# Token-major attention output, accumulated logits and ranks, and later expert weights in a fused attention and mixture-of-experts kernel

## The chip, the cores and the metric

The kernel runs on one core of one Trainium2 chip. The metric is the device time of one execution in microseconds; less is better. Engines: PE (TensorE), DVE (VectorE), ACT (ScalarE), POOL (GpSimd), SP (SyncE).

## The reference

Three parts, one after the other, in FP32:

```python
# decayed linear attention, B, H, S, D = 4, 8, 768, 64
state = gamma * state + k_t v_t^T        # per batch and head
y_t = scale * q_t state
# top-1 mixture of experts on x = y as [3072, 512]; 8 experts, 512 -> 1024 -> 512
logits = x @ w_gate
e_idx = argmax(logits)                   # first of equal ones
gate_w = softmax(logits)[e_idx]
eom = sigmoid(x @ w_output_gate)[e_idx]
x = gate_w * eom * (relu(x @ w1[e_idx]) @ w2[e_idx])
# RMS norm and a gated block, 512 -> 1536 -> 512
out = (silu(xn @ w_gate2) * (xn @ w_val)) @ w_out
```

## The kernel before, in words

The 3072 tokens are cut into 24 chunks of 128, six to a batch. A loop over chunks `n` (L672) runs the attention stage. In iteration `n`, PE does in this order: the scores of chunk n+1 (`qk`, L467: eight matmuls on 64 rows each, the two heads of a pair on two halves of the array), the rows and logits of chunk n-1 (`rows`, L524), the state product of chunk n (`qs_pv`, L490, not in a batch's first chunk), its value product (L495), the state update (`st_up`, L513, not in a batch's last chunk), and the ranks of chunk n-1 (`place`, L555 to L557).

The attention output is feature-major: a head pair's 128 features lie on the partitions and the 128 tokens along the row. `rows` therefore multiplies each of its four blocks with a constant of 144 columns, 128 of the identity and 16 of the two gate matrices. That gives the row of each token and four partial logits, which DVE adds (L529). DVE then finds the largest logit, the first expert that has it, and its one-hot row; `run_cnt` (L544) sums one-hot rows over the chunks. `place` makes the rank of each token within its expert by three small matmuls, weighs the row (L588), stores it to DRAM from ACT's queue, and scatters the token's number into a list by an indirect DMA on POOL.

In FP32 every PE.matmul shows as two LDWEIGHTS (PEld) and two MATMUL records. Expert weights come in 64 pieces of 512 KB; a piece is split into a high and a low half by ACT (L179) and POOL (L180). Eight pieces are loaded and split while the attention stage runs, one in every second chunk (L690 to L692, L704). In the expert loop `convs_to` (L861) asks for further pieces. SP issues nearly all loads in program order, and q, k and v of a chunk use one of four buffers, so a load waits for the chunk four before it.

The rows of the first expert window are collected in two ways: tokens of early chunks are gathered from DRAM (`gather`, L255, four indirect DMAs on POOL) and added by PE with the identity (`settle_in`, L604); tokens of the last three chunks (NDIRECT) are put in place by matmuls with a selection matrix, as a rounded part `rh` and a rest `rl` (`direct_in`, L595). Then `split` (L263, L264) makes the two halves that the first expert's `up` (L285) reads.

The order of the work on each engine is the order in which the code issues it; the tile framework adds the waits. The end of the stage reads:

```python
        direct_in(NCH - 3, True)
        place(NCH - 2)
        rows(NCH - 1)
        settle_in((0, 1))
        place(NCH - 1)
        settle_in((2, 3))
        direct_in(NCH - 2, False)
        direct_in(NCH - 1, False)
```

Of the kernel before, what the change touches and what calls it, by code (L numbers as in the profile page):

```python
# [21 lines left out]
CH = 128  # L22
# [21 lines left out]
NDIRECT = 3  # L44
# [27 lines left out]
def shape_constants():  # L72
# [14 lines left out]
    hd = 2 * np.arange(NP)[None, None, :, None] + (p[:, None, None, None] >= 64)  # L87
    ti = np.arange(CPB)[None, :, None, None] * CH + p[None, None, None, :] + 1.0
    rs = g[hd] ** ti / np.sqrt(D)
# [14 lines left out]
def fused_kernel(  # L104
# [311 lines left out]
    with ExitStack() as es:  # L416
# [3 lines left out]
        rp = pool(es, "rowp", 4)  # L420
# [11 lines left out]
        st_sb = [ap.tile([128, NP, 128], F32, name=f"st{i}") for i in range(2)]  # L432
        run_cnt = ap.tile([128, NCH + 1, NE], BF16, name="run_cnt")
# [3 lines left out]
        a_t, vt_t, am_t, xt_t, row_t, rt, direct = {}, {}, {}, {}, {}, {}, {}  # L437
        scat = []
# [44 lines left out]
        def qs_pv(n):  # L483
            c = n % CPB
            qT = a_t[n][:, 0].rearrange("p (a t) -> p a t", a=NP)
            vt, am = vt_t[n], am_t.pop(n)
            o = ps[:, 4].rearrange("p (a t) -> p a t", a=NP)
            if c:
                for a in range(NP):
                    PE.matmul(  # L490
                        o[:, a], lhsT=st_sb[n % 2][:, a], rhs=qT[:, a], start=(a == 0), stop=True, skip_group_check=True
                    )
            for a in range(NP):
                for i in range(2):
                    PE.matmul(  # L495
                        o[64 * i:64 * i + 64, a], lhsT=vt[:, 2 * a + i], rhs=am[i][:, a],
                        start=(c == 0 and a == 0), stop=True, skip_group_check=True,
                    )
            xt = tp.tile([128, NP, CH], F32, name="xt", tag="xt")
            DVE.tensor_tensor(out=xt, in0=o, in1=rs[:, c], op=ALU.mult)  # L500
            xt_t[n] = xt

        def st_up(n):
# [16 lines left out]
        def rows(n):  # L520
            xt = xt_t.pop(n)
            for k in range(KB):
                o = (k % 2) * 144
                PE.matmul(ps[:, 5 + k // 2, o:o + 144], lhsT=xt[:, k], rhs=iwt[:, k], start=True, stop=True)  # L524
            v = ps[:, 5:7, 0:288].rearrange("p a (b c) -> p a b c", b=2)
            t = rp.tile([128, DM], F32, name="row", tag="row")
            row_t[n] = t
            lg = tp.tile([128, 16], F32, name="lg", tag="lg")
            DVE.tensor_reduce(  # L529
                out=lg, in_=v[:, :, :, 128:144].rearrange("p a b j -> p j a b"), axis=AX.XY, op=ALU.add  # L530
            )
            ACT.activation(
                out=t.rearrange("p (a b c) -> p a b c", a=2, b=2), in_=v[:, :, :, 0:128], func=AF.Copy
            )
            sc = tp.tile([128, 12], F32, name="sc", tag="sc")
            col = [sc[:, i:i + 1] for i in range(12)]
            mx, pm, nmx, sm, nz, ez, s1, t1, gw, pos = col[:10]
            ohb = tp.tile([128, NE], BF16, name="ohb", tag="ohb")
            DVE.tensor_reduce(out=mx, in_=lg[:, 0:8], axis=AX.X, op=ALU.max)
            DVE.scalar_tensor_tensor(out=junk[:, 0], in0=lg[:, 0:8], scalar=mx, in1=prio, op0=ALU.is_ge, op1=ALU.mult)  # L540
            DVE.tensor_scalar(out=nmx, in0=mx, scalar1=-1.0, scalar2=None, op0=ALU.mult)
            DVE.tensor_reduce(out=pm, in_=junk[:, 0], axis=AX.X, op=ALU.max)
            DVE.tensor_scalar(out=ohb, in0=prio, scalar1=pm, scalar2=None, op0=ALU.is_equal)
            DVE.tensor_tensor(out=run_cnt[:, n + 1], in0=run_cnt[:, n], in1=ohb, op=ALU.add)  # L544
            ACT.activation(out=junk[:, 1], in_=lg[:, 0:8], func=AF.Exp, bias=nmx, accum_out=sm)
            DVE.scalar_tensor_tensor(
                out=junk[:, 2], in0=lg[:, 8:16], scalar=-1.0, in1=ohb, op0=ALU.mult, op1=ALU.mult, accum_out=nz
            )
            ACT.activation(out=ez, in_=nz, func=AF.Exp)
            rt[n] = (ohb, ez, sm, s1, t1, gw, pos)  # L550

        def place(n):
            ohb, ez, sm, s1, t1, gw, pos = rt.pop(n)
            rk = ps[:, 7, (n % 2) * 8:(n % 2) * 8 + 8]
# [20 lines left out]
            if n < NCH - 1:  # L575
                store_row(n, t, gw)
            else:
                row_t[n] = (t, gw)
# [30 lines left out]
        def totals_a():  # L609
            PE.matmul(ps[:, 7, 32:40], lhsT=oh, rhs=run_cnt[:, NCH], start=True, stop=True)  # L610
# [456 lines left out]
```

## Time and profile before

| | |
|---|---|
| three runs | 1118.16, 1119.85, 1119.85 us; median 1119.85 |
| the profiled execution | 1119.29 us, of which the span is 1117.2 us |
| busy share of the span | PE 94%, PEld 88%, DVE 49%, ACT 34%, POOL 30% |
| mean granted clock | 0.986 |

Times in the rows are microseconds from the start of the span, means are nanoseconds. "out<-in" names the tiles; "L500" is a line of the kernel. PE and PEld overlap: PEld is the load of the stationary operand, PE the stream of the moving one. The engines' idle time is put down to what ended it. The attention stage ends at about 153 us, the experts run from 173 us on, and the last block from about 460 us to the end.

### The profile page before, as it was taken

The numbers are of one execution on the slowest core, as the hardware profiler recorded it, in microseconds if no ns is written. First come the engines' busy times: TensorE is split into PE (matmuls) and PEld (weight loads), VectorE is DVE, ScalarE is ACT, GpSimd is POOL, SyncE is SP. The second block draws the span as 40 slices with busy tenths as digits, with TensorE's granted clock in tenths as the row PEclk, the third lists the DMA queues.
The fourth block names the chain that finished last, engine by engine and source line by source line (L and its number), as shares of the span: only waits on it lengthen the run. The fifth ranks groups of instructions, "written<-read, shape, count | busy, mean of one in ns | idle before, by whom it ended". The sixth has DMA issues, their size and how long they took to land.

```text
span 1117.2 us, 16379 instructions
## 1 busy us (share of the span) xinstructions
PE 1055.5 (94%) x6393; PEld 982.8 (88%) x6394; DVE 550.9 (49%) x1045; ACT 381.4 (34%) x721; POOL 337.2 (30%) x271
## 2 busy tenths in 40 slices
PE   7788889999999999989899899999999999999995
PEld 6687779989999999978788799999999999999995
DVE  4699963256666676888888831111311112211111
ACT  1344333444444544555555531111311112211111
POOL 3355544556466656332433310000110000200002
PEclk9899989999999999999999999999999999999998
DMA  8999724445446555543343220000210000100001
GB/s 301 229 307 284 204 63 135 123 135 197 155 142 205 182 156 155 171 104 94 114 141 114 85 85 29 1 1 1 64 50 1 1 1 30 57 1 1 1 1 60
DMA packets 47864, 116.74 MB, mean 104 GB/s; under 512 B 12966, under 2 KB 24486, under 8 KB 44962
## 3 DMA queue, kind: packets, MB, share of 16 engines
q1 hardware_dynamic: 39602, 97.05, 28.8%
q0 software_dynamic: 4864, 12.53, 3.2%
q10 hardware_dynamic: 3312, 6.03, 1.6%
q8 instruction: 52, 0.85, 0.3%
q14 instruction: 34, 0.28, 0.1%
HBM read 93.06 MB, written 23.11 MB: 104 GB/s over the span
## 4 chain that ended last, share of the span: by engine, by line
issue 43%; PE 25%; DVE 11%; POOL 3%; DMA 2%; ACT 2%; POOLq 0%; DVEq 0%; SPq 0%; ACTq 0%
PE ps L285 12%; PE ps L298 11%; DVE fb L226 2%; DVE fb L229 2%; POOL out_dram L780 2%; DVE fu L232 1%; DVE fb L223 1%; PE ps L271 1%; DMA out_dram<-ob,perm 1%; DVE a L755 1%; DVE al L757 1%; ACT ah L756 1%; DVE ys L347 1%; PE ps L604 1%; DMA raw<-wm 1%
## 5 line engine op out<-in xcount | busy, mean ns | idle before, releaser
L747 PE MATMUL ps<-zh,w 128*128 128x384 f32 x960 | 255.2, 336 | 2.6 <-DVE hl L292 1.3
L755 DVE TENSOR_TENSOR a<-a,ps 128x384 f32<-128x384 f32 x96 | 52.8, 550 | 320.2 <-PE ps L747 317.7
L180 POOL TENSOR_TENSOR w<-raw,w 128x1024 fp32r<-128x1024 f32 x64 | 154.7, 2426 | 103.0 <-ACT w L179 102.2
L747 PEld LDWEIGHTS ps<-zh,w 128*128 128x128 f32 x960 | 174.6, 188 | 5.7 <-ACT a L754 1.7
L747 PE MATMUL ps<-xh,w 128*128 128x384 f32 x576 | 156.5, 341 | 9.8 <-ACT a L754 7.2
L747 PE MATMUL ps<-zl,w 128*128 128x384 f32 x480 | 161.2, 336 | 0.0
L285 PE MATMUL ps<-xh,w 128*128 128x448 f32 (+7 forms) x512 | 149.6, 353 | 0.1
L765 PE MATMUL ps<-w,ah 128*128 128x512 f32 x564 | 145.5, 393 | 0.2 <-ACT ys L320 0.2
L780 POOL DMA_INDIRECT out_dram<-xw,perm x10 | 9.9, 992 | 423.3 <-ACT xw L778 420.1
L756 ACT ACTIVATE ah<-a 128x384 fp32r<-128x384 f32 x94 | 49.3, 525 | 209.6 <-DVE a L755 209.6
L747 PEld LDWEIGHTS ps<-xh,w 128*128 128x128 f32 x576 | 104.9, 188 | 17.3 <-ACT a L754 11.3
L765 PEld LDWEIGHTS ps<-w,ah 128*128 128x128 f32 x564 | 104.7, 188 | 16.6 <-ACT ys L320 0.6
L754 ACT ACTIVATE a<-ps 128x384 f32<-128x384 f32 x96 | 46.7, 487 | 202.6 <-PE ps L747 202.5
L298 PE MATMUL ps<-hh,w 128*128 128x448 f32 (+7 forms) x512 | 106.6, 350 | 0.0
L285 PEld LDWEIGHTS ps<-xh,w 128*128 128x128 f32 x512 | 95.2, 188 | 3.4
L747 PE MATMUL ps<-xl,w 128*128 128x384 f32 x288 | 96.9, 336 | 0.0
L298 PEld LDWEIGHTS ps<-hh,w 128*128 128x128 f32 x512 | 93.8, 188 | 2.9
L747 PEld LDWEIGHTS ps<-zl,w 128*128 128x128 f32 x480 | 90.1, 188 | 2.3
L285 PE MATMUL ps<-xl,w 128*128 128x448 f32 (+7 forms) x256 | 89.8, 351 | 0.0
L180 POOL TENSOR_TENSOR w<-fu,w 128x512 fp32r<-128x512 f32 x36 | 55.7, 1546 | 111.7 <-ACT w L179 108.2
L765 PE MATMUL ps<-w,al 128*128 128x512 f32 x282 | 80.1, 392 | 0.0
L757 DVE TENSOR_TENSOR al<-a,ah 128x384 fp32r<-128x384 f32 x94 | 52.5, 558 | 55.5 <-ACT ah L756 55.5
(154 smaller groups left out, 1497.9 us busy)
## 6 DMA issues: line engine op xcount, KB each, us to landing
raw<-wmoe SPq DMA_DIRECT2D x64, 512.0 KB, 3.9
qkv<-att SPq DMA_DIRECT2D x22, 1024.0 KB, 8.0
raw<-wm SPq DMA_DIRECT2D x36, 512.0 KB, 3.7
xw<-z SPq DMA_DIRECT2D x8, 768.0 KB, 6.4
xr<-row ACTq DMA_DIRECT2D x23, 256.0 KB, 7.8
z<-ys SPq DMA_DIRECT2D x2, 912.0 KB, 7.6
z<-ys SPq DMA_DIRECT2D x2, 896.0 KB, 4.3
z<-ys SPq DMA_DIRECT2D x2, 864.0 KB
```

The source lines that it names most:

```text
L180: POOL.tensor_tensor(out=dst[:, 1, c], in0=src, in1=f32(dst[:, 0, c]), op=ALU.subtract)
L226: DVE.scalar_tensor_tensor(out=b, in0=lo, scalar=29, in1=b, op0=ALU.logical_shift_right, op1=ALU.bitwise_or)
L229: DVE.scalar_tensor_tensor(out=b, in0=hi, scalar=-(1 << 30), in1=b, op0=ALU.bitwise_and, op1=ALU.bitwise_or)
L285: PE.matmul(p, lhsT=wtile[:, s, k * 128:(k + 1) * 128], rhs=x[w % len(xh)][:, k, 0:n], start=(i == 0), stop=(i == 3 * KB - 1),)
L298: PE.matmul(ps[:, 4 + k, 0:n], lhsT=wtile[:, s, 512 + k * 128:512 + (k + 1) * 128], rhs=h, start=(f == 0 and j == 0), stop=(f == NF - 1 an ...
L747: PE.matmul(ps[:, part, 0:BT], lhsT=w2(f, part, s, k * 128, (k + 1) * 128), rhs=zz[:, k], start=(i == 0), stop=(i == 3 * KB - 1),)
L754: ACT.activation(out=a, in_=ps[:, 0, 0:BT], func=AF.Silu)
L755: DVE.tensor_tensor(out=a, in0=a, in1=ps[:, 1, 0:BT], op=ALU.mult)
L756: ACT.activation(out=ah, in_=a, func=AF.Copy)
L757: DVE.tensor_tensor(out=al, in0=a, in1=f32(ah), op=ALU.subtract)
L765: PE.matmul(ps[:, o_bank[b % 2][t]], lhsT=x[:, t * 128:(t + 1) * 128], rhs=w2(f, 2, s, 0, 512), start=(f == 0 and j == 0), stop=(f == NF2 ...
L780: ins = POOL.indirect_dma_start(out=out[:, :], out_offset=bass.IndirectOffsetOnAxis(ap=pm[:, t0 + t], axis=0), in_=o, in_offset=None, boun ...
```

## The change

The attention output is made token-major. The value product now has the masked scores as its stationary operand (128 columns) and the scaled values (64 columns) as the moving one; the state product has q as the stationary operand and the state, no longer padded to a 128x128 block, as the moving one. DVE scales it straight into the row. For the logits, the row is turned by four transposes (`turn_row`), copied by ACT, and multiplied with 16 columns, the four blocks accumulating in PSUM (`logits`). The logits are negated in the constant, so that the largest becomes the smallest. The ranks of all chunks accumulate in one place in PSUM (`rank`): each chunk adds what the chunk before left out and its own part, and `run_cnt` goes. The row stage takes one more chunk: choosing the expert of chunk n-1 and weighing chunk n-2 are issued on DVE in turn. Chunk n-2 is placed in iteration n. The state is copied whole by ACT. Weight pieces are loaded from chunk 20 on; three are split in the stage, the rest behind the first window. Four chunks instead of three go by `direct_in`, the gather comes in the last iteration, and the last two chunks are ranked before the gathered rows are added.

```diff
-NDIRECT = 3
+NDIRECT = 4
...
-        rp = pool(es, "rowp", 4)
+        rp = pool(es, "rowp", 6)
...
-        rs = ap.tile([128, CPB, NP, CH], F32, name="rs")
-        iwt = ap.tile([128, KB, 144], F32, name="iwt")
+        rs = ap.tile([128, CPB * H], F32, name="rs")
+        iwt = ap.tile([128, KB, 16], F32, name="iwt")
+        rest = ap.tile([128, 128], BF16, name="rest")
-        st_sb = [ap.tile([128, NP, 128], F32, name=f"st{i}") for i in range(2)]
+        st_sb = [ap.tile([128, NP, D], F32, name=f"st{i}") for i in range(2)]
+        ranks = ps[:, 7, 0:8]
...
-            o = ps[:, 4].rearrange("p (a t) -> p a t", a=NP)
+            o = ps[:, 4:6, 0:NP * D].rearrange("p g (a e) -> p g a e", a=NP)
             if c:
-                for a in range(NP):
+                for h in range(H):
+                    r = 64 * (h % 2)
                     PE.matmul(
-                        o[:, a], lhsT=st_sb[n % 2][:, a], rhs=qT[:, a], start=(a == 0), stop=True, skip_group_check=True
+                        o[:, h % 2, h // 2], lhsT=qT[r:r + 64, h // 2], rhs=st_sb[n % 2][r:r + 64, h // 2],
+                        start=(h < 2), stop=True, skip_group_check=True,
                     )
...
+            for h in range(H):
+                PE.matmul(
+                    o[:, h % 2, h // 2], lhsT=am[h % 2][:, h // 2], rhs=vt[:, h], start=(c == 0 and h < 2), stop=True,
+                    skip_group_check=True,
+                )
+            t = rp.tile([128, DM], F32, name="row", tag="row")
+            a = c * H
+            DVE.tensor_tensor(
+                out=t.rearrange("p (a g e) -> p g a e", a=NP, g=2), in0=o,
+                in1=rs[:, a:a + H].rearrange("p (g a o) -> p g a o", g=2, o=1).to_broadcast([128, 2, NP, D]), op=ALU.mult,
+            )
+            row_t[n] = t
...
-            ACT.activation(out=s[0:64, :, 0:64], in_=v[0:64], func=AF.Copy)
-            DVE.tensor_copy(out=s[64:128, :, 64:128], in_=v[64:128])
+            ACT.activation(out=s, in_=v, func=AF.Copy)
+
+        def turn_row(n):
+            x = ps[:, 6].rearrange("p (k t) -> p k t", k=KB)
+            for k in range(KB):
+                PE.transpose(x[:, k], row_t[n][:, k * 128:(k + 1) * 128], ident)
+            xt = tp.tile([128, KB, CH], F32, name="xt", tag="xt")
+            ACT.activation(out=xt, in_=x, func=AF.Copy)
+            xt_t[n] = xt
+
+        def logits(n):
+
             xt = xt_t.pop(n)
+            lg = ps[:, 6, 0:16]
             for k in range(KB):
...
+                PE.matmul(lg, lhsT=xt[:, k], rhs=iwt[:, k], start=(k == 0), stop=(k == KB - 1))
...
+        def rank(n):
+
+            if n:
+                PE.matmul(ranks, lhsT=rest, rhs=rt[n - 1][2], start=False, stop=True, skip_group_check=True)
+            else:
+                PE.matmul(ranks, lhsT=oh[0:1], rhs=e3[0:1], start=True, stop=True, skip_group_check=True)
+            PE.matmul(ranks, lhsT=uh, rhs=rt[n][2], start=False, stop=True, skip_group_check=True)
+
+        def choose(n):
+            lg, sc, ohb = rt[n]
+            nm, pm, sm, nz, ez = [sc[:, i:i + 1] for i in range(5)]
+
+            def chosen():
+                DVE.tensor_scalar(out=ohb, in0=prio, scalar1=pm, scalar2=None, op0=ALU.is_equal)
+                ACT.activation(out=junk[:, 1], in_=lg[:, 0:8], func=AF.Exp, scale=-1.0, bias=nm, accum_out=sm)
+
+            def gate():
+                DVE.scalar_tensor_tensor(
+                    out=junk[:, 2], in0=lg[:, 8:16], scalar=1.0, in1=ohb, op0=ALU.mult, op1=ALU.mult, accum_out=nz
+                )
+                ACT.activation(out=ez, in_=nz, func=AF.Exp)
...
+            if n < NCH - 2:
+                store_row(n)
...
-            if n == NCH - 2:
+            if n == NCH - 1:
                 ex.gather(0, CAPS[0], NT - NDIRECT * CH)
             qk(n + 1)
             if n >= 1:
-                rows(n - 1)
+                turn_row(n - 1)
             qs_pv(n)
+            if n >= 2:
+                rank(n - 2)
+            if n >= 1:
+                logits(n - 1)
             st_up(n)
-            if 1 <= n < NCH - 1:
-                place(n - 1)
-            if n == NCH - 3:
+            in_turn(choose(n - 1) if n >= 1 else [], weigh(n - 2) if n >= 2 else [])
+            if n >= 2:
+                place(n - 2)
+            if n == NCH - NDIRECT + 1:
                 ex.load_list(0, CAPS[0], 0)
-            if n >= 3 and n % 2 == 1:
-                convs_to((n - 3) // 2)
-                loads_to((n - 3) // 2 + 2)
-        direct_in(NCH - 3, True)
+            if n >= NCH - 4:
+                loads_to(n - NCH + 5)
+                convs_to(n - NCH + 4)
+        direct_in(NCH - 4, True)
+        turn_row(NCH - 1)
+        rank(NCH - 2)
+        direct_in(NCH - 3, False)
+        logits(NCH - 1)
+        in_turn(choose(NCH - 1), weigh(NCH - 2))
         place(NCH - 2)
-        rows(NCH - 1)
-        settle_in((0, 1))
+        rank(NCH - 1)
+        in_turn(weigh(NCH - 1))
         place(NCH - 1)
-        settle_in((2, 3))
         direct_in(NCH - 2, False)
-        direct_in(NCH - 1, False)
+        last = CAPS[0] // 128 * 128
+        settle_in(range(0, last, 128))
         for k in range(KB):
+            settle_in(range(last, CAPS[0], 128), (k,))
+            direct_in(NCH - 1, False, (k,))
             ex.split(0, k, CAPS[0], ps[:, k, 0:CAPS[0]])
-        store_row(NCH - 1, *row_t[NCH - 1])
-        convs_to(NPRE)
+        store_row(NCH - 2)
+        store_row(NCH - 1)
...
-            convs_to(min(t + NSLOT - 3, NPRE + max(0, t - 1) * 3 // 2))
+            convs_to(min(t + NSLOT - 3, 4 + t * 3 // 2))
```

## Rows read from the trace of the kernel before

**Rows 1.** Stretches: length; PE, PEld, DVE, ACT, POOL busy; PEclk; DMA; GB/s.

```profile
54.80:116.20 61.40, 51.74 (x701) 46.84 (x698) 57.89 (x200) 27.29 (x69) 32.76 (x35) 1.00 0.97 287
116.20:119.60 3.40, 3.40 (x18) 3.18 (x19) 3.23 (x14) 1.55 (x4) 2.11 (x3) 0.50 0.85 243
157.20:170.80 13.60, 11.62 (x40) 9.48 (x41) 2.37 (x12) 1.69 (x5) 4.48 (x8) 0.50 0.15 46
```

**Rows 2.** One chunk of PE in order of time: start, length, group, instructions.

```profile
22.49 1.16 PE L467 MATMUL ps<-qkv 64*128 64x128 f32 x16
23.59 1.25 PE L524 MATMUL ps<-iwt,xt 128*128 128x144 f32 x8
24.67 1.05 PE L490 MATMUL ps<-qkv,st 128*128 128x128 f32 x8
25.65 1.09 PE L495 MATMUL ps<-am,vt 128*64 128x128 f32 x16
26.58 0.63 PE L513 MATMUL ps<-vt,qkv 128*64 128x64 f32 x16
27.14 0.17 PE L555 MATMUL ps<-e,oh 1*128 1x8 bf16 x1
27.39 1.16 PE L467 MATMUL ps<-qkv 64*128 64x128 f32 x16
```

**Rows 3.** DVE in order of time, L500 of chunks 1 and 23.

```profile
21.90 0.69 DVE L500 TENSOR_TENSOR xt<-ps,rs 128x512 f32<-128x512 f32 x1 [1.25 <-PE ps L495]
...
152.97 0.69 DVE L500 TENSOR_TENSOR xt<-ps,rs 128x512 f32<-128x512 f32 x1
```

**Rows 4.** Waits from 20 to 160 us: in total, times, longest.

```profile
ACT row L532 <- DVE lg L529: 22.6, 15, 8.1
...
PE ps L467 <- DMA qkv<-att: 9.6, 4, 6.9
```

**Rows 5.** DVE's L544 in order of time, beside a weight split and alone.

```profile
124.19 2.30 DVE L544 TENSOR_TENSOR run_cnt<-run_cnt,ohb 128x8 bf16<-128x8 bf16 x1
...
131.39 0.16 DVE L544 TENSOR_TENSOR run_cnt<-run_cnt,ohb 128x8 bf16<-128x8 bf16 x1
```

**Rows 6.** Weight loads by line, 60 to 150 us: busy us, mean ns.

```profile
L524 PEld LDWEIGHTS ps<-iwt,xt 128*128 128x128 f32 x128 | 17.0, 193 | 11.2 <-ACT st L517 10.2
...
L513 PEld LDWEIGHTS ps<-vt,qkv 128*64 128x64 f32 x224 | 8.4, 138 | 0.0
```

**Rows 7.** PE by shape, 157 to 170 us: busy us, mean ns.

```profile
L604 PE MATMUL ps<-cs,xw 128*128 128x128 f32 x24 | 7.3, 460 | 3.8 <-DMA xw<-xr,ix 3.8
L604 PE MATMUL ps<-cs,xw 64*128 64x64 f32 x8 | 2.7, 445 | 0.0
```

**Rows 8.** Transposes of the first expert stage in order of time.

```profile
200.29 0.95 PE L271 MATMUL ps<-cs,xw 128*128 128x128 f32 x8
```

**Rows 9.** ACT by line, 60 to 150 us: busy us, mean ns.

```profile
L517 ACT ACTIVATE st<-ps 64x256 f32<-64x256 f32 x14 | 5.1, 362 | 0.4 <-PE ps L513 0.4
L545 ACT ACTIVATE junk<-lg,sc 128x8 f32<-128x8 f32 x16 | 4.7, 296 | 4.8 <-DVE sc L541 4.8
```

**Rows 10.** The attention stage's end in order of time, three engines.

```profile
150.21 0.72 ACT L572 ACTIVATE rh<-row,sc 128x512 fp32r<-128x512 f32 x1 [1.37 <-DVE sc L563]
...
150.97 0.75 DVE L573 SCALAR_TENSOR_TENSOR rl<-row,sc,rh 128x512 fp32r<-128x512 f32 x1 [0.37 <-ACT rh L572]
...
173.34 0.47 PE L285 MATMUL ps<-xh,w 128*128 128x448 f32 x1
```

**Rows 11.** The first expert in order of time, POOL and PE.

```profile
182.15 1.04 POOL L255 DMA_INDIRECT xw<-xr,ix  x1 [15.77 <-DMA ix<-lst]
...
187.18 2.42 POOL L180 TENSOR_TENSOR w<-raw,w 128x1024 fp32r<-128x1024 f32 x1
...
190.52 0.37 PE L285 MATMUL ps<-xh,w 128*128 128x448 f32 x1
```

**Rows 12.** PE in chunk 1 in order of time.

```profile
16.89 2.29 PE L524 MATMUL ps<-iwt,xt 128*128 128x144 f32 x8
```

More of the change, by code (lines that the diff above doesn't have):

```diff
@@ L521, in rows @@
+        def logits(n):
             xt = xt_t.pop(n)
+            lg = ps[:, 6, 0:16]
             for k in range(KB):
[L523 to L540, printed above, removed]
@@ new lines, in weigh @@
+        def weigh(n):
+            lg, sc, ohb = rt[n]
+            sm, nz, ez, s1, t1, gw, pos = [sc[:, i:i + 1] for i in range(2, 9)]
+            ii = tp.tile([128, 1], I32, name="ii", tag="ii", bufs=3)
+            rt[n] = (lg, sc, ohb, gw, pos, ii)
+            return [
+                lambda: DVE.tensor_scalar(out=s1, in0=sm, scalar1=1e-9, scalar2=None, op0=ALU.add),
+                lambda: DVE.scalar_tensor_tensor(
+                    out=junk[:, 3], in0=ranks, scalar=1.0, in1=ohb, op0=ALU.mult, op1=ALU.mult, accum_out=pos
+                ),
+                lambda: DVE.tensor_scalar(out=t1, in0=ez, scalar1=1.0, scalar2=s1, op0=ALU.add, op1=ALU.mult),
+                lambda: DVE.tensor_copy(out=ii, in_=pos),
+                lambda: DVE.reciprocal(out=gw, in_=t1),
+            ]
@@ L579, in place, with in_turn @@
+        def in_turn(*lists):
+            for i in range(max(len(x) for x in lists)):
+                for x in lists:
+                    if i < len(x):
+                        x[i]()
+        def place(n):
+            gw, pos, ii = rt[n][3:]
             ins = POOL.indirect_dma_start(
@@ L598, in direct_in, with settle_in @@
                     )
[L600 to L602 removed]
+        def settle_in(ts, ks=range(KB)):
+            for t0 in ts:
+                for k in ks:
                     r = min(128, CAPS[0] - t0)
@@ L609, in totals_a @@
         def totals_a():
-            PE.matmul(ps[:, 7, 32:40], lhsT=oh, rhs=run_cnt[:, NCH], start=True, stop=True)
+            PE.matmul(ranks, lhsT=rest, rhs=rt[NCH - 1][2], start=False, stop=True, skip_group_check=True)
         def totals_b():
             cnt = ap.tile([1, 1, 8], F32, name="cnt")
-            DVE.tensor_copy(out=cnt, in_=ps[0:1, 7, 32:40].rearrange("p (o e) -> p o e", o=1))
+            DVE.tensor_tensor(
+                out=cnt, in0=ranks[0:1].rearrange("p (o e) -> p o e", o=1),
+                in1=ca[0:1, A_E3:A_E3 + 8].rearrange("p (o e) -> p o e", o=1), op=ALU.subtract,
+            )
             s3 = [1, 8, 8]
@@ L657, in fused_kernel @@
         SP.dma_start(out=cs, in_=cst)
-        SP.dma_start(out=rs[:, 1], in_=rsc[:, 1])
         DVE.tensor_copy(out=uh, in_=ca[:, A_U:A_U + 128])
+        DVE.tensor_scalar(out=rest, in0=ca[:, A_U:A_U + 128], scalar1=-1.0, scalar2=1.0, op0=ALU.mult, op1=ALU.add)
         DVE.memset(oh, 1.0)
@@ L663, in fused_kernel @@
         DVE.tensor_copy(out=ids, in_=ca[:, A_IDS:A_IDS + NCH])
-        DVE.memset(run_cnt[:, 0], 0.0)
+        DVE.tensor_scalar(out=iwt, in0=iwt, scalar1=-1.0, scalar2=None, op0=ALU.mult)
         fill = {
```

95 lines of the change are left out of this document (31 added, 64 removed).

## The prediction, made before the change had run

> **What bounds the kernel now.** I first cut the span into stages by the granted clock (the view by stretches), then laid out one chunk of the attention stage in order of time, then read the groups by line and tile shape, last the list of waits. From 170.8 us on TensorE is full for the first experts, so an edit there costs nothing until it is late. In the attention stage two engines share the bound: in 54.8 to 116.2 us DVE is busy 57.89 of 61.40 us and PE 51.74 [rows 1]. An undisturbed chunk is bound by PE alone: from one L467 to the next, 22.49 to 27.39, are 4.90 us in which every PE group follows the last without a gap [rows 2]. The real chunks are longer: chunk 1's product on DVE (L500) starts at 21.90 and chunk 23's at 152.97, which is 131.1 us for 22 chunks, 5.96 each [rows 3]. The difference is waits: PE stood 9.6 us for the q/k/v transfers [rows 4], and in the chunks that carry a weight split a small DVE operation beside that split on POOL takes 2.30 us where it takes 0.16 alone (L544) [rows 5].
>
> **What decides the change: weight loads.** In FP32 each PE.matmul is two load/matmul pairs. A load of 128 columns lasts 193 ns and one of 64 columns 138 [rows 6]; so 64 columns are 55 ns and a load of 128 is about 110 ns of work behind a fixed latency, an estimate from these two rows. Today it hides: a matmul with 128 moving columns streams as long (L490: 8 of them from 24.67 to 25.65, 0.12 each [rows 2]). The change keeps 128 weight columns and cuts the moving side to 64 (state and value products) or 16 (logits). The nearest row is L604 at half clock: its 64x64 form, under weights of 128 columns, takes 445 ns where the 128x128 form takes 460 [rows 7]. Halving the moving columns gave nearly nothing. I therefore take 0.11 us for every new matmul instruction. The ends are 0.06 (half of the 0.12 above, were loads hidden) and 0.12. The Trainium skill ("TensorE: Matmul & The Clock Gate", "Back-to-back issue gap") prices an isolated matmul by its moving columns alone; by that rule the sum would be some 33 us lower, which is the second rival below, and L604's row speaks against it.
>
> **PE per chunk, before against after** [rows 2]. Scores: 1.10, unchanged. L524 (1.08) goes; four transposes (eight of them take 0.95 at L271 with the tail of the last [rows 8], so about 0.11 each) with 0.15 of switching to the half-array form are 0.58. State product: 0.98 becomes 16 instructions in pairs on two halves of the rows, as in L467, 1.03. Value product: 0.93 becomes 16 x 0.11 + 0.06 = 1.82, since two column halves no longer run side by side. Logits: 8 x 0.11 + 0.1 = 0.97. Ranks: three small matmuls (0.25) become two, 0.12. State update 0.56 becomes 0.60 with the switch. Sum 6.22 against 4.90.
>
> A wait joins it. The turned row and the logits share one PSUM bank, so the next transposes wait until DVE's gate operation has read the logits. The gate must follow ACT's exponential, since reads of one bank by ACT and DVE are kept apart (today ACT's L532 waits 22.6 us for DVE's L529, which reads the same banks [rows 4]), and in ACT's queue the exponential (0.30) stands behind the state's copy (0.36) [rows 9], which waits for the state update. From the end of the logits that is 0.60 + 0.2 of latency + 0.36 + 0.30 + about 0.5 for the accumulator's read and the gate = 1.96; PE gets there after 0.60 + 1.10 = 1.70. So PE waits 0.25, with the state product, the value product and all later matmuls queued behind it; ends 0 and 0.6. The chunk is 6.47. First chunks of a batch (three of them in the 22) lack the state product, -1.1; last ones lack the update, -0.2. 22 x 6.47 - 3.9 = 138.4, against 131.1: **+7.3 us**. Chunk 1 runs at half clock: ahead of its product on DVE, turning saves 1.1 us (2.29 for L524 at 16.89 [rows 12], against twice 0.58) and the value product adds 1 to 2.7, the more the longer the clock stays low; I take **+1**.
>
> **What leaves the other engines.** DVE loses L544, half of the state copy, the logits' reduction and a negation per chunk; it stood at 5.6 us of 5.96 (57.89 of 61.40 [rows 1]) and only gets shorter, so with PE at 6.47 this is worth nothing beyond what the sum holds. Five of eight weight splits leave ACT and POOL with the stalls that they caused. The eight weight loads leave the middle of the stage; four are issued on SP in the last four chunks, behind the last of the q/k/v loads, so nothing of the stage waits for them. The other 1.5 MB of constants that go (rs, iwt) make room for q, k and v, which have two chunks, 13 us, to land.
>
> **End of the stage.** From chunk 23's L500 to the first expert matmul are 152.97 to 173.34, 20.4 us [rows 3, 10]. After: a weight split is queued on ACT ahead of the copy of each late row, the list and the gather come one chunk later (ranks are placed two chunks behind) and stand on POOL behind a weight split, and the last two chunks go in series through choice, weighing, rh (0.72) and rl (0.75) [rows 10] before the gathered rows are added, where today those additions fill the wait. I count 14 us to the last rl, PE at direct_in(22) until about then, then L604's 32 instructions (10.0 us at half clock [rows 7], 5 at full) with eight of L595 in between: 21 to 28 us, and I take 25, because the clock was at half in just this stretch [rows 1] and the new order has idle PE before it: **+4.6**.
>
> **First expert.** Five more splits come behind the first window. The tight one is weight 4: POOL's four gathers begin at 182.15 after waiting for the list, a split can begin at 187.18 and takes 2.42, and up(4) starts 17.2 us after the first expert matmul (190.52) [rows 10, 11]. It is ready at 189.6: 0.9 us of margin, cost 0, bounds 0 and +5. On SP the weight loads stand behind the list's load as now.
>
> **Clock.** Some stretches at half clock: I take **+2**; the low end is 0, the high end is the first rival.
>
> The sum is 7.3 + 1 + 4.6 + 2 = +14.9 on the profiled execution's own 1119.29 us (span 1117.2; 0.05% under the median 1119.85): **1134 us**. Its own range: 1121 (no wait, short end) to 1150.
>
> **Rivals.**
> *Half clock in the loop.* At 116.2 to 119.6 the clock was granted at 0.50 right after a chunk with PE waits, and at 157.2 to 170.8 it stayed at 0.50 although PE was busy 11.62 of 13.60 us with short matmuls [rows 1]: being busy in the rows isn't enough to hold 2.4 GHz. In the new chunk PE streams during only about half of its time, the rest is loads. Half clock doubles it (L524: 2.29 at 16.89 against 1.25 [rows 2, 12]), 6.0 us per chunk: a third of the chunks gives 7.3 x 6.0 = +44, 1176; all of them about 1265. Against it: from 54.8 to 116.2 the clock was 1.00 with PE idle for 16% of the time [rows 1]. The Trainium skill ("TensorE: Matmul & The Clock Gate", Part 4) says that transposes do not count as PE activity in the way matmuls do; by that the new transposes make this case likelier, and no row here separates it.
> *Faster: loads hide after all.* If a 64-column matmul cost half of a 128-column one, pv, state product and logits would lose 1.65 us, PE's chunk would be 4.6 and the wait for the gate would grow to about 0.5: 5.0 x 22 - 3 = 107, 24 us less in the loop, with the end and the start as above 1119.3 - 24 + 5.6 = 1101. It decides at a price per instruction of about 0.09 us: 32 slots per chunk at 0.02 less are 0.6 us, 14 in the loop, which pays the rest. For it: L513's 16 instructions, both sides 64, take 0.56 [rows 2]. Against it: L604 [rows 7].
> *Weights late*: the POOL margin of 0.9 us goes and up(4) waits: +5 on the forecast, 1139.
> *No change*: the switches cost nothing, the chunk comes to 5.9 and the end to 21: within 2 us.
>
> **How the numbers follow.** The forecast has 0.48, half clock 0.27, weights late 0.06: slower 0.81. Hidden loads have 0.13, all faster. No change 0.06. About 0.2% (2.2 us) is what a measurement of this kernel can tell from none. The range 1112 to 1182 leaves out most of the hidden loads (0.09) and the half-clock cases with more than a third of the loop (0.11). The likeliest case's own range is 1121 to 1150.
>
> **What the changed profile would show.** Right: value-product matmuls 0.11 us apart with PE's weight-load row nearly full, DVE well under PE in the attention stage, PE waiting before the transposes for the gate, last product on DVE near 161, first expert matmul near 186, then PE full. Wrong: value product at 0.9 to 1.0 us per chunk, or DVE still above 90%; a granted clock under 0.85 between 25 and 160 us decides for the first rival; a PE wait at up(4) for POOL's split for the third.

## The result, and the profile after

The changed kernel took 1129.8 us (median of 20 runs, 1123.24 to 1145.26) against 1119.2 us before (median of 20, 1117.47 to 1120.9). The ratio is 1.009, 95% interval 1.0073 to 1.0106: slower, by 10.6 us of median. The profiled execution took 1125.7 us with a span of 1123.7 at a mean granted clock of 0.991, so it is 4.1 us under the median, and its span is 6.5 us over that of before (1117.2). The longest run, 1145.26 us, counts as a slow one and is not in the ratio; the other eighteen have mean granted clocks of 0.981 to 0.988, all under the profiled one's 0.991, so the rows below show less time at the lower clock than most executions had.

First the three instants of [rows 3, 10], in order of time (start, length, engine, line):

```profile
20.48 0.69 DVE L502 TENSOR_TENSOR row<-ps,rs 128x512 f32<-128x512 f32 x1 [2.47 <-PE ps L496]
...
154.53 0.69 DVE L502 TENSOR_TENSOR row<-ps,rs 128x512 f32<-128x512 f32 x1 [2.08 <-PE ps L496]
...
179.48 0.45 PE L284 MATMUL ps<-xh,w 128*128 128x448 f32 x1
```

They split the 6.5 us. Chunk 1's product on DVE starts 1.4 us earlier than before (20.48, 21.90). From chunk 1 to chunk 23 are 134.05 us instead of 131.07: +3.0. From there to the first expert matmul are 24.95 instead of 20.37: +4.6. From that matmul to the end of the span are 944.2 instead of 943.9: +0.3. So the whole loss of this execution lies in the attention stage and its end. Below, the stretch from chunk 1 to chunk 23 is called the loop, the one from there to the first expert matmul the tail, and time at a granted clock of 0.50 half clock.

One ordinary chunk of PE, in order of time, to lay beside [rows 2]:

```profile
94.17 1.16 PE L467 MATMUL ps<-qkv 64*128 64x128 f32 x16
95.27 0.66 PE L527 MATMUL ps<-cs,row 128*128 128x128 f32 x4
95.85 1.11 PE L491 MATMUL ps<-st,qkv 64*128 64x64 f32 x16
96.89 2.00 PE L496 MATMUL ps<-vt,am 128*128 128x64 f32 x16
98.72 0.17 PE L545 MATMUL ps<-ohb,rest 128*128 128x8 bf16 x1
98.75 0.17 PE L548 MATMUL ps<-ohb,uh 128*128 128x8 bf16 x1
98.78 1.04 PE L537 MATMUL ps<-iwt,xt 128*128 128x16 f32 x8
99.75 0.69 PE L518 MATMUL ps<-vt,qkv 128*64 128x64 f32 x16
100.37 1.16 PE L467 MATMUL ps<-qkv 64*128 64x128 f32 x16
```

Read the starts, not the lengths, which overlap. From start to start: scores 1.10, turning 0.58, state product 1.04, value product (L496) 1.83 for 16 instructions, that is 0.114 each, ranks 0.06, logits 0.97, state update 0.62. No line has an idle time in brackets: PE sets the pace, at 6.20 us a chunk, where the undisturbed chunk of before had 4.90. The loop got only 3.0 us longer because before, its chunks were seldom undisturbed. The stretches by granted clock, with the columns of [rows 1]:

```profile
17.10:105.80 88.70, 87.40 (x1071) 81.15 (x1070) 46.35 (x207) 28.07 (x82) 28.60 (x40) 1.00 0.81 210
105.80:109.20 3.40, 3.40 (x35) 3.02 (x36) 1.24 (x14) 1.45 (x5) 1.79 (x3) 0.50 1.04 246
109.20:157.00 47.80, 44.83 (x543) 41.62 (x543) 23.99 (x108) 17.25 (x45) 17.54 (x23) 1.00 0.65 190
157.00:160.40 3.40, 3.40 (x12) 3.09 (x12) 2.21 (x14) 1.17 (x4) 2.94 (x3) 0.50 0.48 121
160.40:167.30 6.90, 3.86 (x25) 2.96 (x23) 2.92 (x13) 2.62 (x5) 5.69 (x6) 0.99 0.43 122
167.30:174.10 6.80, 5.82 (x19) 5.06 (x20) 2.87 (x13) 1.54 (x3) 2.20 (x4) 0.50 0.04 4
```

DVE, which was busy 57.89 of 61.40 us [rows 1], is now busy 46.35 of 88.70, and PE 87.40. The granted clock fell to 0.50, the lower level (1.2 GHz), at 105.8 us, in a chunk in which PE had no wait before it. That chunk lasted 7.67 us instead of 6.19: 1.48 us for one such stretch. In the end of the stage it was 0.50 twice more.

The end of the stage, four engines, each in order of time:

```profile
156.31 1.26 PE L537 MATMUL ps<-iwt,xt 128*128 128x16 f32 x8 [1.79 <-ACT xt L529]
...
167.10 0.17 PE L548 MATMUL ps<-ohb,uh 128*128 128x8 bf16 x1 [1.96 <-DVE ii L585]
168.24 0.74 PE L625 MATMUL ps<-pt,rh 128*128 128x448 f32 x1 [0.97 <-ACT rh L609]
...
171.80 4.30 PE L634 MATMUL ps<-cs,xw 128*128 128x128 f32 x26
...
154.71 1.06 ACT L178 ACTIVATE w<-raw 128x1024 fp32r<-128x1024 f32 x1 [1.52 <-DMA raw<-wmoe]
155.68 0.58 ACT L529 ACTIVATE xt<-ps 128x512 f32<-128x512 f32 x1
...
165.08 1.97 DVE L555 TENSOR_SCALAR ohb<-ca,sc 128x8 bf16<-128x8 f32 x1
...
170.27 0.75 DVE L611 SCALAR_TENSOR_TENSOR rl<-row,sc,rh 128x512 fp32r<-128x512 f32 x1 [0.44 <-ACT rh L609]
...
164.67 2.34 POOL L179 TENSOR_TENSOR w<-raw,w 128x1024 fp32r<-128x1024 f32 x1
```

At 156.31 PE had waited 1.79 us for the copy of the turned row (L529), which stood on ACT behind a weight split (L178) that itself had waited for its transfer. At 167.10 it had waited 1.96 us for the choice of chunk 23: DVE's L555 took 1.97 us beside POOL's split at 164.67, where it takes 0.23 elsewhere. The gathered rows (L634) come last, though POOL had issued the last of their gathers at 162.33.

### The profile page after: what moved, and what is told of

It is laid out like the page before. It is cut to its first block, busy times and chain, and to the rows that moved or that the text cites. A ratio compares the mean times of both kernels' runs of the same rounds, so it can differ in the third digit from the quotient of the medians.

```text
span 1123.7 us, 16753 instructions
## 1 busy us (share of the span) xinstructions
PE 1081.5 (96%) x6633; PEld 1008.7 (90%) x6634; DVE 511.5 (46%) x956; ACT 380.4 (34%) x722; POOL 337.0 (30%) x269
## 4 chain that ended last, share of the span: by engine, by line
issue 45%; PE 31%; DVE 13%; POOL 4%; DMA 3%; ACT 3%; SPq 0%; POOLq 0%; DVEq 0%; ACTq 0%
PE ps L284 10%; PE ps L297 10%; PE ps L496 3%; DVE fb L225 2%; DVE fb L228 2%; POOL out_dram L821 2%; PE ps L537 2%; PE ps L467 2%; DVE fu L231 2%; PE ps L491 1%; DVE fb L222 1%; POOL w L179 1%; PE ps L270 1%; PE ps L527 1%; DMA out_dram<-ob,perm 1%
```

## The experiments

Theory: PE's chunk is set by loads of 128 weight columns, and the tail by its order. Rivals: stretches at half clock make the loss; the weight part makes it; the tail is long because of the clock alone. Ratios are to the kernel before, measured beside each.

### The value product with twice the moving columns

```diff
-            o = ps[:, 4:6, 0:NP * D].rearrange("p g (a e) -> p g a e", a=NP)
+            o = ps[:, 4:6].rearrange("p g (a w) -> p g a w", a=NP)
...
+                m = min(2, H - h)
                 PE.matmul(
-                    o[:, h % 2, h // 2], lhsT=am[h % 2][:, h // 2], rhs=vt[:, h], start=(c == 0 and h < 2), stop=True,
+                    o[:, h % 2, h // 2, 0:m * D], lhsT=am[h % 2][:, h // 2],
+                    rhs=vt[:, h:h + m].rearrange("p m e -> p (m e)"), start=(c == 0 and h < 2), stop=True,
                     skip_group_check=True,
                 )
```

> The changed kernel, with the moving side of the value product widened from 64 to 128 columns for seven of eight heads (the second half is the next head's, goes to unused columns of the two banks and is read by nobody). Theory of the prediction, that the loads of 128 weight columns set the pace: 14 instructions go from 0.114 to at most 0.12 us, so the value product goes from 1.83 to 1.95 us at most, the ordinary chunk from 6.19 to 6.3, the time stays within 2 to 3 us of the changed kernel's 1129.8. Rival, that the moving columns set it: 14 x 0.055 = 0.77 us per chunk, 17 us in the loop, about 1147. Third, that the wide spread of the changed kernel (1123 to 1145) is stretches at half clock that come where PE streams little: then the widened kernel, which streams more in the same time, spreads less and its median falls to 1123 to 1127.

1123.21 us (9 runs, 1122.01 to 1125.71), ratio 1.003 (1.0019 to 1.0041). One chunk of PE, in order of time:

```profile
95.53 1.11 PE L491 MATMUL ps<-st,qkv 64*128 64x64 f32 x16
96.57 2.00 PE L497 MATMUL ps<-vt,am 128*128 128x128 f32 x16
98.40 0.17 PE L547 MATMUL ps<-ohb,rest 128*128 128x8 bf16 x1
```

The value product takes 1.83 us as before the widening (96.57 to 98.40), the chunk 6.19. Seven of eight heads stream twice the columns at no cost, so the moving columns do not set the pace; the rival by them (+17 us) is out. A fixed price for each instruction is out too: the 16 instructions of the state update, with 64 weight columns each, take 0.62 us in the ordinary chunk above. What is left are the loads of 128 weight columns. What did change is the clock: the stretch at 105.8 is gone,

```profile
105.80:109.20 3.40, 3.40 (x54) 2.98 (x53) 2.48 (x14) 2.05 (x6) 2.11 (x3) 1.00 0.99 183
```

with no half clock between 17 and 155.8 us. The nine executions have mean clocks of 0.989 to 0.992 where the changed kernel's, without the longest, have 0.981 to 0.991; the median fell by 6.6 us, and the intervals of the ratios (1.003 and 1.009) lie apart. The third theory holds too: the two are not exclusive. The two kernels below that add to this one keep the clock as well, with one stretch at half clock in their two loops together, while three further traces of the token-major loop without the added columns have five to seven each. How the one brings the other is left open: the half clock went when these columns were added, with the outputs laid out wider in their two banks for it and nothing else moved on PE.

### The four combinations of products and weights

The weight part alone, put into the kernel before:

```diff
-            if n >= 3 and n % 2 == 1:
-                convs_to((n - 3) // 2)
-                loads_to((n - 3) // 2 + 2)
+            if n >= NCH - 4:
+                loads_to(n - NCH + 5)
+                convs_to(n - NCH + 4)
...
-        convs_to(NPRE)
...
-            convs_to(min(t + NSLOT - 3, NPRE + max(0, t - 1) * 3 // 2))
+            convs_to(min(t + NSLOT - 3, 4 + t * 3 // 2))
```

> The kernel before, with only the weight part of the change: no weight load or split in chunks 3 to 19, one load more and one split in each of the last chunks, the others behind the first windows, as in the changed kernel. Theory, that PE's 4.9 us per chunk is the floor and the 131.1 us of the loop hold waits for transfers (9.6 us) and DVE stalls beside splits (about 1 us per chunk): chunk 1 to 23 takes 110 to 119 us, the tail grows by 2 to 4 us, the time falls to 1103 to 1112. Rival, that DVE's own work (57.9 of 61.4 us) sets the pace: 125 to 131 us, and with the longer tail 1117 to 1123.

1110.49 us, ratio 0.9915 (0.9901 to 0.993). The loop takes 122.67 us, 8.4 less than before, and the tail 20.47. The time lies in the theory's range, but both expectations missed the loop, which lies between them, and the tail did not grow by the 2 to 4 us expected. PE still waits for q, k and v, 7.7 us in three waits.

The same diff, reversed, in the changed kernel:

> The changed kernel, with only its weight part undone: eight loads and splits in chunks 3 to 19 as in the kernel before, none in the last four chunks, none ahead of schedule behind the first windows. Theory, that with the token-major products PE sets the chunk (6.19 us) and DVE has room: the splits cost nothing in the loop (chunk 1 to 23 at 133 to 138 us), the tail loses the split waits (22 to 23 us), time within 4 us of the changed kernel's 1129.8; the weight part, which is worth 9 us in the kernel before, is worth nothing here. Rival, that the stalls beside splits and the transfers' contention come back as before: chunk 1 to 23 at 142 us or more, 1138 or more.

1137.98 us, ratio 1.0194 (1.0152 to 1.0236). The theory failed here: the loop takes 146.0 us, not 133 to 138; the tail, 20.7 us, is below its 22 to 23. The stretch of that loop, columns as above:

```profile
22.00:168.00 146.00, 143.00 (x1604) 132.15 (x1603) 71.09 (x325) 51.88 (x137) 66.20 (x74) 0.90 0.78 207
```

The rival's sizes fit, its reason does not: PE is busy 143 of 146 us, so the 12 us are not idle time: the granted clock is 0.90 on average, and seven stretches at half clock (the last one reaching into the tail) lie in the loop where the changed kernel's profile has one. How much of the 12 us the splits bring, one trace does not tell: the changed kernel's own loop took 144.6 us, with five stretches, in the trace of `rows_first` below, whose edit acts only behind the loop. The medians differ by 8.2 us, from four runs of 1134.75 to 1149.03 us here.

The token-major products alone undone, all else as changed, except that for space three chunks go by `direct_in` and the rows have five buffers:

```diff
-            lg = ps[:, 6, 0:16]
             for k in range(KB):
-                PE.matmul(lg, lhsT=xt[:, k], rhs=iwt[:, k], start=(k == 0), stop=(k == KB - 1))
+                o = (k % 2) * 144
+                PE.matmul(ps[:, 5 + k // 2, o:o + 144], lhsT=xt[:, k], rhs=iwt[:, k], start=True, stop=True)
...
-            if n >= 1:
-                turn_row(n - 1)
+            if n >= 1:
+                logits(n - 1)
             qs_pv(n)
             if n >= 2:
                 rank(n - 2)
-            if n >= 1:
-                logits(n - 1)
```

The functions `qs_pv` and `st_up`, the constants and the copies out of PSUM are those of the kernel before.

> The changed kernel, with only the token-major output undone: value product, state product and row products are feature-major with 144 columns as before, choice and weighing in turn, ranks summed in PSUM, weights late, order of the tail as changed (three direct chunks and five row buffers, for space). Theory, that the token-major products alone make the chunk 6.2 us on PE: the chunk falls to 4.9 to 5.2, chunk 1 to 23 to 107 to 115 us, tail 22 to 25, time 1098 to 1108. Rival, that the chunk is held by something else in the change (ranks in series, order on DVE, the clock): chunk 5.8 to 6.2, time 1118 to 1130.

1110.04 us, ratio 0.9909 (0.9893 to 0.9925). The loop takes 115.9 us, 18 less than the changed kernel's; its undisturbed chunks 4.94 us. The list of PE's waits in its loop:

```profile
PE ps L468 <- DMA qkv<-att: 8.6, 5, 2.8
```

and a stretch of it, where PE has 2.8 us idle and the DMA engines are busy 0.97 of the time:

```profile
60.00:95.00 35.00, 32.19 (x420) 28.79 (x420) 24.45 (x117) 14.84 (x41) 14.49 (x21) 1.00 0.97 243
```

Medians of the four: feature-major 1119.2 with splits in the loop and 1110.5 with late weights, token-major 1138.0 and 1129.8. By these the weight part is worth 8 to 9 us on either; the token-major part (with the new ranks and tail, which came with it in these four) costs about 19 on either. The hybrid tells the products apart from ranks and tail: undoing them gives back 20 us. Half clock is not the main part of this: the widened kernel has none in its loop, which still takes 132.6 us, while the loops of the kernel before with late weights (122.7) and of the hybrid (115.9) hold some.

### The tail

```diff
-            if n >= NCH - 4:
-                loads_to(n - NCH + 5)
-                convs_to(n - NCH + 4)
+            if 12 <= n < 20:
+                loads_to((n - 8) // 2)
+            if n >= 14 and n % 2 == 1 and n < 20:
+                convs_to((n - 12) // 2)
```

> The changed kernel, with the loads and splits of the first three weights in chunks 14 to 19 in place of the last four chunks. Theory, that the splits queued ahead of the late rows cost 3 to 4 of the 4.6 us by which the tail grew (two waits of the logits for a split on ACT, 1.8 and 0.9 us, and one small DVE operation of 1.97 us beside the split on POOL): the tail from chunk 23's product on DVE to the first expert matmul goes from 24.95 to 21 or 22 us, the loop stays within 2 us because PE sets its pace, and the time falls by 2 to 4 us. Rival, that the tail is the series of choice, weighing and rows at half clock: 24 to 25 us as now, no difference. Second rival, that splits within the loop still stall the chunks through DVE: the loop grows by up to 3 x 2.2 us and eats the gain.

1130.49 us, ratio 1.0097 (1.0068 to 1.0127): no gain. The tail is 22.9 us, shorter by 2 but not the 21 to 22 expected, and the choice of chunk 23 has no stall any more (DVE, in order of time):

```profile
174.91 0.23 DVE L555 TENSOR_SCALAR ohb<-ca,sc 128x8 bf16<-128x8 f32 x1
```

but the loop of that execution is 143.2 us, with six stretches at half clock and a seventh at its end. Three of the six, at 29, 50 and 80 us, lie ahead of the first moved load and split, so it was not these that brought them: the changed kernel's own loop can have them.

The gathered rows earlier:

```diff
         place(NCH - 2)
+        last = CAPS[0] // 128 * 128
+        settle_in(range(0, last, 128))
         rank(NCH - 1)
...
         direct_in(NCH - 2, False)
-        last = CAPS[0] // 128 * 128
-        settle_in(range(0, last, 128))
```

> The changed kernel, with the 12 full tiles of the gathered rows added right after the weighing of chunk 22, ahead of chunk 23's ranks, in place of after chunk 22's direct rows. Theory, that PE in the tail waits for the choice and the rows of the late chunks (2.0 and about 1.4 us) and that this work, 4.3 us at mixed clock, fills the wait as in the kernel before: the tail goes from 24.95 to 21 to 23 us, the time falls by 2 to 4 us. Rival, that the gathered rows land too late or that chunk 23's ranks, now behind them, become the end: tail 24 to 27 us, no gain.

1130.68 us (1120.58 to 1137.01), ratio 1.0077 (1.0044 to 1.011). The tail of the profiled execution is 16.9 us, its loop 144.6 us with five stretches at half clock and a sixth at its end. The median shows nothing, but the three fastest runs (1120.58 to 1121.3) are below all twenty of the changed kernel. The half clock in the loop, which this edit does not touch, can hide what the order gives, so I repeated the test on the widened kernel, whose loop keeps its clock; the edit is the two diffs together:

> The changed kernel with both repairs: value product widened to 128 moving columns, and the 12 full tiles of the gathered rows ahead of chunk 23's ranks. Theory, that the changed kernel's loss is two separate things, stretches at half clock in the loop (widening took 6.6 us off the median) and PE waits in the tail (25.0 us against 16.9 with the rows first, in a run whose loop was at half clock for more of the time): the loop stays at 132 to 134 us, the tail is 17 to 20 us, time 1115 to 1119. Rival, that the earlier rows only moved the half clock from the tail into the last chunks of the loop: 1121 to 1124, as with the widening alone.

1118.41 us in eleven of its twelve executions, ratio 0.9987 (0.9977 to 0.9997); the twelfth took 3709.74 us, with no cause that the records show (with it the median is 1118.66). The interval lies below the widened kernel's, so here the earlier rows give 4 to 5 us. The loop is 132.6 us, the tail 21.7 against the widened kernel's 25.3. The expected times hold; the tail is longer than the 17 to 20 expected.

With the diff of the early splits on top:

> Both repairs, and the first three weights loaded and split in chunks 14 to 19 in place of the last four. Theory, that splits in the loop cost through the PE waits that they make, which bring half clock in the chunks after (splits_in_loop: 47 us at half clock in the profiled run against 23): 1 to 6 us slower than both repairs alone. Rival, that PE's own pace hides them and the tail loses its split waits: 1 to 2 us faster.

1117.56 us, ratio 0.9976 (0.9961 to 0.9991). The intervals overlap: by the medians the early splits are worth about 1 us, which is not told apart from none. The theory missed in its sum: the splits do lengthen the loop by 4.7 us (137.3), 1.6 of it in the last chunk, at half clock, but they shorten the tail by 6.1 (15.65). The tails as stretches, columns as above; the widened kernel, then with the rows first, then with both:

```profile
152.70:178.00 25.30, 19.40 (x90) 15.84 (x90) 10.80 (x40) 8.38 (x17) 12.46 (x12) 0.80 0.29 77
```

```profile
151.65:173.40 21.75, 17.07 (x90) 13.00 (x90) 10.85 (x40) 8.51 (x17) 12.45 (x12) 0.92 0.34 91
```

```profile
156.10:171.70 15.60, 14.67 (x89) 11.72 (x88) 8.37 (x40) 6.03 (x14) 6.09 (x9) 1.00 0.28 58
```

The same work on PE: its idle time goes from 5.9 to 4.7 to 0.9 us, the mean clock from 0.80 to 0.92 to 1.00 and PE's busy time from 19.4 to 14.7. That each wait brings the half clock is not shown, though. At the head of the first two tails PE waits about equally long for the turned row; chunk 23's logits follow later (widened kernel, then with the rows first):

```profile
154.16 1.06 PE L539 MATMUL ps<-iwt,xt 128*128 128x16 f32 x8 [1.43 <-ACT xt L531]
...
160.89 1.06 PE L539 MATMUL ps<-iwt,xt 128*128 128x16 f32 x8 [0.17 <-ACT xt L531]
```

```profile
153.29 1.06 PE L539 MATMUL ps<-iwt,xt 128*128 128x16 f32 x8 [1.64 <-ACT xt L531]
...
160.03 1.06 PE L539 MATMUL ps<-iwt,xt 128*128 128x16 f32 x8 [1.02 <-ACT xt L531]
```

The clock fell to 0.50 for 3.4 us between the two in the first, not in the second, and the logits start 8.2 and 8.4 us behind chunk 23's product: here the half clock only filled time that PE would have waited. The gain of the earlier rows lies behind that point (17.14 us from there to the first expert matmul became 13.35), in waits and half clock together, and these three tails do not separate the two.

### Looking for the best version

The hybrid with the gathered rows earlier, by the diff above:

> The hybrid (feature-major products, all else as changed, no lean constants) with the 12 full tiles of the gathered rows ahead of chunk 23's ranks. Theory: its tail, 22.6 us with 3.0 and 0.9 us of PE waits and half clock, falls to 18 to 20 us, time 1105 to 1108. Rival, that chunk 23's ranks, now queued behind the tiles, end the tail: 22 us or more, 1109 to 1112.

1110.9 us, ratio 0.9909 (0.989 to 0.9927), the hybrid's own. Its profiled tail is 24.0 us, against 22.6, with 13.7 us of it at half clock; the gain did not carry over. The theory missed, and not for the rival's reason: PE waited for the rows themselves, which had not landed:

```profile
152.89 5.49 PE L632 MATMUL ps<-cs,xw 128*128 128x128 f32 x24 [3.41 <-DMA xw<-xr,ix]
```

The hybrid with fewer constants to load (and `cs` loaded earlier):

```diff
-        SP.dma_start(out=iwt, in_=iw)
+        SP.dma_start(out=iwt[:, :, 128:144], in_=iw[:, :, 128:144])
...
+                POOL.tensor_tensor(
+                    out=rs[:, n + 1], in0=rs[:, n],
+                    in1=ca[:, A_G:A_G + NP].rearrange("p (a o) -> p a o", o=1).to_broadcast([128, NP, CH]), op=ALU.mult,
+                )
```

> The hybrid (feature-major products, everything else as changed) with 1.5 MB fewer constants: the identity is copied on the chip in place of four copies in memory, and the row scales of chunks 1 to 5 are made on POOL from those of chunk 0. Theory, that what the hybrid's loop (115.9 us) still holds above 22 x 4.94 - 4.5 = 104 us are the waits for the q/k/v transfers (8.6 us) beside these constants, and the half clock after them: loop 106 to 111 us, time 1101 to 1106. Rival, that the transfers are late for their own 1 MB per 4.94 us: the wait only moves to a later chunk, loop 114 to 117 us, time 1108 to 1111.

1111.64 us, ratio 0.992 (0.9895 to 0.9945): no gain. The theory missed, and the rival in its sizes: the loop grew to 120.1 us, the tail to 26.3. PE's waits for q, k and v grew to 11.2 us in seven waits, and from 66 to 95 us the DMA engines are busy all the time. The longest wait did not move: it grew in the chunk in which the hybrid has its second longest (the hybrid, then this kernel).

```profile
53.34 1.46 PE L468 MATMUL ps<-qkv 64*128 64x128 f32 x16 [2.65 <-DMA qkv<-att]
```

```profile
54.85 2.08 PE L470 MATMUL ps<-qkv 64*128 64x128 f32 x16 [4.07 <-DMA qkv<-att]
```

And with the diff of the early splits on top:

> The same with the first three weights loaded and split in chunks 14 to 19 in place of the last four. Theory: the tail, 22.6 us in the hybrid, falls to 20.5 us or less, and DVE, at about 4 of 4.94 us, absorbs most of the splits: time 1 to 3 us under the kernel without this. Rival: three loads of 0.5 MB make q/k/v late and the stalls beside splits lengthen three chunks by 1 to 2 us each, no gain or 2 to 4 us lost.

1113.24 us, ratio 0.9933 (0.9914 to 0.9953). The tail fell to 19.95 us and the loop rose to 124.1: the rival, with no gain; the 1.6 us lost by the medians lie within the intervals.

So the best versions are the kernel before with late weights and the hybrid, 1110.5 and 1110.0 us, which the intervals don't tell apart. PE's longest waits in both loops are those for q, k and v (7.7 and 8.6 us); no run here removed them.

## Why the prediction was right, and where its terms were off

The forecast of 1134 us stands against 1129.8, within the likeliest case's own range of 1121 to 1150, and for the reason given: the loads make the chunk. That it came so near is in part luck. The profiled execution took 1125.7 us, 8.4 less than the sum; the median lies nearer because most executions, by their mean clocks, had more half clock than that one. Of the signs, the spacing and DVE's room came; the wait before the turning came in five chunks only, and chunk 23's product lies at 154.53 instead of 161, the first expert matmul at 179.48 instead of 186. By its steps:

**Price of a load: right, and shown.** 0.11 us for each new matmul instruction became 0.114 in the value product, and the widened kernel shows that it is the load. The row that the prediction leaned on, L604 with 445 against 460 ns [rows 7], could only hint at it: these are lengths of records, which overlap. The Trainium skill ("TensorE: Matmul & The Clock Gate", "LDWEIGHTS (loading the stationary operand)") gives a load's time in ns as its columns over 1.2, which is 107 for 128; the spacing of 0.114 at full clock agrees within 7%. At half clock the spacing is 0.217, which that formula, with no clock in it, does not give (`rows_first`, granted clock 0.50):

```profile
164.39 3.67 PE L496 MATMUL ps<-vt,am 128*128 128x64 f32 x16
167.86 0.21 PE L545 MATMUL ps<-ohb,rest 128*128 128x8 bf16 x1
```

The Trainium skill ("TensorE: Matmul & The Clock Gate", "Back-to-back issue gap") says that in a stream load and matmul together set the spacing; in the rows here it was the load, up to 128 moving columns. The formula for an isolated matmul in the same section of the Trainium skill, from which the 33 us came, does not fit here.

**PE per chunk: right.** 6.22 us were summed and 6.19 measured, each piece within 0.06. The 0.15 and 0.04 us for switching to the half-array form stand in no row by themselves; the pieces that hold them came out at 0.58 and 0.62.

**The wait for the gate, +0.25 a chunk: wrong.** The step added the state update, a latency, the state's copy, the exponential, and the accumulator's read with the gate end to end, 1.96 us; the 0.2 of latency and the 0.5 at the end stood in no row. PE, ACT and DVE between the logits and the next turning:

```profile
93.56 0.69 PE L518 MATMUL ps<-vt,qkv 128*64 128x64 f32 x16
...
94.29 0.38 ACT L522 ACTIVATE st<-ps 128x256 f32<-128x256 f32 x1 [3.51 <-PE ps L518]
...
94.57 0.26 ACT L556 ACTIVATE junk<-ps,sc 128x8 f32<-128x8 f32 x1
...
94.95 0.17 DVE L559 SCALAR_TENSOR_TENSOR junk<-ps,ohb 128x8 f32<-128x8 f32 x1 [0.27 <-ACT junk L556]
95.05 0.08 DVE L559 DVE_READ_ACCUMULATOR junk<-ps,ohb 128x1 f32 x1
```

The chain takes 1.57 us, from 93.56 to 95.13; the exponential starts only 0.28 after the copy, though the copy's row is 0.38 long. PE gets to the turning at 95.27, straight after the scores. PE waited for L559 five times, 2.5 us in all. That took about 22 x 0.25 - 2.5 = 3.0 of the predicted +7.3 out.

**Loop.** With it gone, 22 x 6.22 - 3.9 + 2.5 = 135.4 against 134.0 measured, which hold one stretch at half clock (1.5). Of the 2.9 us that are then left, 0.7 are 6.19 in place of 6.22, and 1 is the first chunk of a batch, 4.65 to 5.01 us where the sum has 5.12. The rest is not accounted for. The widened kernel's loop, with the same chunk and no half clock, takes 132.6, which is the 134.0 less that stretch.

**Chunk 1, +1: not confirmed; the -1.4 is no sure effect of the change either.** The granted clock stands at 1.00 here in both profiles, so only the lengths of like instructions tell the level. In this execution PE was at the higher one by the state product of chunk 1, which starts at 17.41 and takes 1.11 us, the length of later chunks; before, L524 at 16.89 still took 2.29 [rows 12]:

```profile
14.61 2.08 PE L467 MATMUL ps<-qkv 64*128 64x128 f32 x16
16.62 0.86 PE L527 MATMUL ps<-cs,row 128*128 128x128 f32 x4
17.41 1.11 PE L491 MATMUL ps<-st,qkv 64*128 64x64 f32 x16
18.45 2.00 PE L496 MATMUL ps<-vt,am 128*128 128x64 f32 x16
```

Before, PE waited 2.03 us for q, k and v ahead of these scores, and now it did not; but that isn't the reason. The kernel before with late weights, whose first chunks are the same code, waited as long and ran its scores in 1.16 us, the length of later chunks (the kernel before, then with late weights):

```profile
14.88 2.08 PE L467 MATMUL ps<-qkv 64*128 64x128 f32 x16 [2.03 <-DMA qkv<-att]
```

```profile
14.64 1.16 PE L467 MATMUL ps<-qkv 64*128 64x128 f32 x16 [2.00 <-DMA qkv<-att]
```

And `rows_first`, whose start is the changed kernel's, did not wait and still had this value product at double length:

```profile
19.77 3.67 PE L496 MATMUL ps<-vt,am 128*128 128x64 f32 x16
```

With the same code, chunk 1's product on DVE starts at 21.90 or 18.95 before, at 20.48 or 23.48 after: the start moves by some 3 us from one execution to the next, more than either figure.

**Tail, +4.6: right to 0.1 us, in part by luck.** The split queued ahead of the late rows, the series of the last two chunks and the gathered rows left to the end are each in the rows above. But the last rl ended 16.5 us behind chunk 23's product (171.02) where 14 were counted, and what followed took 8.5 where the 25 us left 11. Half clock behind PE's idle time came as the prediction had it; that the one brings the other is not shown.

**First expert, 0: right.** +0.3 us.

**Clock, +2: too small in the median.** The profiled execution has one stretch in its loop, 1.5 us; the same loop in `rows_first` has five and took 144.6 us. The widened kernel is 6.6 us faster at the same chunk time, so half clock costs the median of the changed kernel about that much, by this account; no row here is of a median execution. This is the first rival's mechanism in a small size; the prediction kept them apart as two cases where they came together. The missing gate wait and the undersized clock nearly cancel.

**"Worth nothing beyond what the sum holds", of the splits that leave the loop: right as bookkeeping, misleading as a price.** With the splits back in the loop the median is 8.2 us higher, a gain that the prediction never named. And it missed the larger point, that this part alone makes the kernel before 9 us faster.

## What to carry to other kernels

Before swapping the operands of an FP32 matmul, count weight columns loaded per result: a product whose moving side is shorter than its 128 weight columns pays for the load, and narrowing the moving side further saves nothing. When a change bundles several parts, price the one that takes work out of a shared stage against the old kernel too; here it was the whole gain, and the other part cost about twice that. In a tail, fill PE's waits with work that has landed: the gathered rows moved forward shortened one tail by 3.6 us, and lengthened another by 1.4, where their transfer was not done.

## What the runs showed that I had not expected

Streaming unused columns made a kernel faster: 1123.2 instead of 1129.8 us, with the clock's mean going from 0.981 to 0.991 (the longest run aside) up to 0.989 to 0.992 over the runs. The third theory ahead of that run allowed for it; the prediction did not. And a busy PE does not keep the higher level: the changed kernel lost it at 105.8 us after 88.7 us in which PE was busy 87.4, and the kernel with splits in the loop ran 143 of 146 us busy at a mean clock of 0.90.
